# Threshold attention and a feed-forward block on one core: inputs laid out for the matmuls, work moved between engines, batch 0 in half jobs

## The chip, the cores and the metric

The kernel runs on one core of a Trainium2 chip. A core has five engines with a queue of instructions each: TensorE (PE in the profile) multiplies matrices, VectorE (DVE), ScalarE (ACT) and GpSimd (POOL) work elementwise, and SyncE (SP) here issues all the transfers between main memory and the on-chip memory SBUF. Matmul results lie in PSUM, which VectorE and ScalarE can read and GpSimd in this kernel never does. Each engine works off its queue in order. The metric is the device time of one execution in microseconds.

## The reference

Eight batches, eight heads, 576 tokens, 64 values per head. Scores are scaled by 1/8; those more than `tau` = 0.02 under the maximum of their row are dropped before the softmax:

```python
scores = scale * np.matmul(q, k.transpose(0, 1, 3, 2))
thresh = np.max(scores, axis=-1, keepdims=True) - tau
scores = np.where(scores >= thresh, scores, -1000000000.0)
scores = scores - np.max(scores, axis=-1, keepdims=True)
attn = np.exp(scores)
attn = attn / (np.sum(attn, axis=-1, keepdims=True) + 1e-09)
attn_out = np.matmul(attn, v)
```

The heads are put side by side (512 values per token), and a feed-forward block follows, in which each token is mixed with the one before it:

```python
xk = mu_k * x + (1.0 - mu_k) * x_prev
xr = mu_r * x + (1.0 - mu_r) * x_prev
k = np.maximum(xk @ w_k, 0.0)
v = k * k @ w_v
r = 1.0 / (1.0 + np.exp(-(xr @ w_r)))
return r * v
```

`w_k` is 512 x 1024, `w_v` 1024 x 512, `w_r` 512 x 512. The three weights come as 64-bit words of doubles; `mu_r` and `w_r` are about eight times as large as the others, so the gate is sensitive to small errors in attention.

## The kernel before

**Precision by splitting.** TensorE takes one pass over operands of type float32r. To keep near float32 precision an operand x becomes an upper part hi (x rounded to float32r, a ScalarE copy) and a lower part lo = x - hi, and products are summed as hi·hi + hi·lo + lo·hi. Every split costs a copy and a subtraction; where TensorE would be idle, plain float32 matmuls are used instead, which take several passes and need no split (the `whole` job for scores, the `plain` jobs for probabilities by values).

**Jobs and slots.** A job is one batch and two heads; there are 32. It has nine query tiles: four of 128 queries for each head, and one ("T") with the last 64 queries of both heads. Each tile is a slot, so there are 288 slots. A tile runs through a pipeline of five slots:

- `scores` (L308 float32, L326 split): matmuls into the double-buffered PSUM tile `s`, 128 x 576;
- `row_max` (L338, VectorE): the negated maximum of the row; `threshold` (L342, ScalarE): maximum minus tau; `expo` (L346, ScalarE): exponentials into `p`, a tile with three buffers;
- one slot later `mask` (L351, VectorE): p times (s >= threshold), with the sum of the row; `denom` and `inverse` (L355, L358, VectorE): 1e-9 added, reciprocal; `norm` (L361, GpSimd): p times the reciprocal;
- two slots later `turn_p` (L368): five transposes on TensorE into the single PSUM tile `pt`;
- three slots later `p_hi` (L393, or L390 for a plain job; ScalarE) and `p_lo` (L403, VectorE) evacuate `pt` as upper and lower parts into groups of two tiles;
- four slots later `attend` (L439) multiplies a group by the values, or `attend_tile` (L412) one tile of a plain job; `attend_out` (L447, L449, L456) puts the result, transposed, into `xT` or, for the last 64 tokens, `xE`.

**Operands of a job.** While a job runs, the next one's are made: `load` (L158 to L166, eight transfers) and `load_v` (L173, L178, three transfers), transposes of q and k on TensorE (`turn`, L189, nine of them), evacuation with the split (`evac_q`, `evac_k`: ScalarE L206, L209, L219, L222, VectorE L212, L225, GpSimd L210, L223), `stack` (L238 to L241, eight transfers inside SBUF that put upper and lower parts on top of each other), `bd_fill` (L249) and `v_split` (L263, L277, L278). `PREP` tells in which of the nine slots each of these is issued.

**Weights.** Twenty pieces of 128 x 512. `weight_steps` (L128 to L146) turns the words of doubles into float32 with integer operations and splits them, one step a slot and a new piece every second slot from slot 4 on.

**Feed-forward.** Chunks of 256 tokens: two per batch and two for the last 64 tokens of four batches, 18 in all. A chunk has 20 steps on TensorE: eight for `h` (L525, 12 matmuls of 256 columns), four for `z` and eight for `vps` (six of 512 columns each). Ahead of them lie 18 small steps of mixing (`mix`, L485 to L510), in which GpSimd subtracts, adds and splits and ScalarE scales. After each pair of `h` steps `h_out` runs: ReLU (L551, ScalarE), square (L554, VectorE), upper part (L557, ScalarE), lower part (L558, GpSimd).

**The order.** `slot(n)` writes the instructions of one slot in one of two orders (before and from slot `N0` on). ScalarE keeps that written order (`manual_schedule`); the other queues are ordered by the library's scheduler, by its own estimates of durations. How many feed-forward steps go into a slot is a credit: each slot gets `TSLOT` (3.325) minus the estimated TensorE time of its attention work, and each step takes `TSTEP` (1.3) from it; a credit that can't be used is lost. `KEEP` steps stay in hand until the last chunk is ready. A chunk is ready four slots after the last tile of its tokens; the very first chunk then takes eleven slots, one mixing step each, until its steps may begin. What is left after the last slot runs at the end.

## Time and profile before

Three runs: median 1151.09 us, 1151.04 to 1152.42.

| | us | share of the span |
|---|---|---|
| profiled execution, first to last instruction | 1151.2 | |
| median of the runs | 1151.09 | |
| TensorE busy, matmuls (weight loads) | 1104.4 (999.1) | 96% (87%) |
| VectorE busy | 961.3 | 84% |
| ScalarE busy | 846.0 | 73% |
| GpSimd busy | 673.3 | 58% |
| 16 DMA engines, queue 1 | | 38.8% |

The profiled execution is as long as the median run, so durations from it can be put against the median as they are. Busy times overlap and don't add up to the span. Matmuls are pipelined, so the duration in a matmul's row contains time in which the next one already runs. A row of a view by line names the line, the engine, the operation, the tiles (out<-in), the shapes and the count; then the busy time in us and the mean of one in ns; then how long the engine was idle just before these instructions, and what ended that. A row of a timeline starts with its start and length in us.

### The profile page before, as it was taken

The page shows a single profiled execution, that of the slowest core. Times are in us where ns is not written, and L with a number is a line of the kernel's source. Part 1 is how long each engine was busy: PE and PEld are TensorE (multiplying, and loading weights), DVE is VectorE, ACT ScalarE, POOL GpSimd, SP SyncE. Part 2 cuts the span into 40 slices and gives each one's busy share as a digit, 9 for nine tenths or more (in the row PEclk, how much of TensorE's full clock was granted, in tenths as well). Part 3 has the DMA queues.
Part 4 walks back from the last instruction along what each step waited for, and adds up shares of the span by engine and source line. Part 5 has one row for each costly group of instructions (what it writes and reads, how often), then busy time and mean ns, then how long its engine had stood idle before and what let it go on. Part 6 is the DMA issues. An engine that isn't in the chain of part 4 may idle for free.

```text
span 1151.2 us, 22514 instructions
## 1 busy us (share of the span) xinstructions
PE 1104.4 (96%) x7454; PEld 999.1 (87%) x7454; DVE 961.3 (84%) x2399; ACT 846.0 (73%) x1775; POOL 673.3 (58%) x860
## 2 busy tenths in 40 slices
PE   6999989999999999989999999999999999999998
PEld 4887878898989898988989898989898989898997
DVE  3899998888989898988989898989898989895222
ACT  3787877778687878768777878787878787876442
POOL 1465677465656465645747575656565656564672
PEclk9999999999999999999999999999999999999999
DMA  5777334433344344433334444423344444300000
GB/s 131 184 205 204 83 85 93 113 85 74 70 95 105 84 112 95 112 88 71 83 83 104 92 104 104 99 68 87 79 102 94 104 98 99 76 29 13 25 20 18
DMA packets 125027, 105.61 MB, mean 92 GB/s; under 512 B 93681, under 2 KB 101873, under 8 KB 124913
## 3 DMA queue, kind: packets, MB, share of 16 engines
q1 hardware_dynamic: 124912, 104.18, 38.8%
q8 instruction: 60, 0.98, 0.3%
q14 instruction: 55, 0.44, 0.1%
HBM read 39.85 MB, written 9.44 MB: 43 GB/s over the span
## 4 chain that ended last, share of the span: by engine, by line
PE 65%; DVE 18%; ACT 10%; issue 4%; SPq 1%; DMA 1%; POOL 1%; DVEq 0%; ACTq 0%; POOLq 0%
PE h L525 12%; PE vps L525 12%; PE pt L368 10%; PE s L326 9%; PE o L439 9%; PE z L525 8%; DVE p L351 4%; DVE sm L338 3%; DVE plo L403 2%; ACT phi L393 2%; ACT p L346 2%; DVE r L554 2%; PE o L412 1%; DVE phi L403 1%; DVE xT L137 1%
## 5 line engine op out<-in xcount | busy, mean ns | idle before, releaser
L361 POOL TENSOR_SCALAR p<-p,sm 128x576 f32<-128x576 f32 x288 | 222.6, 773 | 255.2 <-DVE sm L358 187.4
L393 ACT ACTIVATE phi<-pt 128x640 fp32r<-128x640 f32 (+1 forms) x270 | 172.4, 649 | 111.3 <-PE pt L368 110.6
L351 DVE SCALAR_TENSOR_TENSOR p<-s,sm,p 128x576 f32<-128x576 f32 x288 | 233.7, 811 | 23.4 <-ACT p L346 19.1
L338 DVE TENSOR_REDUCE sm<-s 128x1 f32<-128x576 f32 x288 | 215.9, 750 | 21.2 <-PE s L308 10.3
L525 PE MATMUL h<-xk,wk 128*128 128x256 f32 x1728 | 231.8, 285 | 1.0 <-ACT r L551 0.3
L525 PE MATMUL vps<-wv,k 128*128 128x512 f32 x864 | 227.2, 399 | 2.0 <-DVE sg L616 1.8
L368 PE MATMUL pt<-ident,p 128*128 128x128 f32 x1440 | 210.4, 276 | 18.6 <-DVE phi L403 8.9
L525 PEld LDWEIGHTS h<-xk,wk 128*128 128x128 f32 x1728 | 216.0, 191 | 4.1 <-ACT r L551 2.1
L346 ACT ACTIVATE p<-s,sm 128x576 f32<-128x576 f32 x288 | 212.6, 738 | 1.4
L368 PEld LDWEIGHTS pt<-ident,p 128*128 128x128 f32 x1440 | 168.2, 142 | 45.9 <-issue 13.5
L403 DVE TENSOR_TENSOR plo<-pt,phi 128x512 fp32r<-128x512 f32 (+1 forms) x270 | 170.5, 632 | 39.6 <-ACT phi L393 33.7
L525 PEld LDWEIGHTS vps<-wv,k 128*128 128x128 f32 x864 | 154.2, 188 | 29.1 <-DVE sg L616 2.9
L439 PE MATMUL o<-phi,vs 128*128 128x256 f32 (+1 forms) x540 | 156.1, 312 | 2.5 <-ACT phi L393 1.6
L439 PE MATMUL o<-plo,vs 128*128 128x256 f32 (+1 forms) x432 | 118.7, 296 | 0.2 <-DVE plo L403 0.2
L326 PE MATMUL s<-st 128*128 128x288 f32 x496 | 112.1, 308 | 5.0 <-DVE p L351 4.2
L558 POOL TENSOR_TENSOR k<-r,k 128x512 fp32r<-128x512 f32 x72 | 93.2, 1295 | 35.6 <-ACT k L557 35.1
L525 PE MATMUL z<-wr,xr 128*128 128x512 f32 x432 | 112.8, 400 | 0.1
L326 PE MATMUL s<-st,st 128*128 128x288 f32 x496 | 107.4, 298 | 0.1
L439 PEld LDWEIGHTS o<-phi,vs 128*128 128x128 f32 x540 | 101.8, 189 | 5.3 <-ACT phi L393 3.3
L342 ACT ACTIVATE sm<-sm,ntau 128x1 f32<-128x1 f32 x288 | 84.5, 293 | 20.8 <-DVE sm L338 19.1
L554 DVE TENSOR_TENSOR r<-r 128x512 f32<-128x512 f32 x72 | 76.8, 1066 | 27.0 <-ACT r L551 26.5
L326 PEld LDWEIGHTS s<-st 128*128 128x128 f32 x496 | 81.8, 191 | 17.4 <-DVE p L351 9.5
(91 smaller groups left out, 1792.5 us busy)
## 6 DMA issues: line engine op xcount, KB each, us to landing
st<-hi SPq DMA_DIRECT2D x62, 288.0 KB, 3.3
st<-lo SPq DMA_DIRECT2D x62, 288.0 KB, 4.1
st<-hi SPq DMA_DIRECT2D x62, 144.0 KB, 3.9
st<-lo SPq DMA_DIRECT2D x62, 144.0 KB, 4.2
raw<-in_q SPq DMA_DIRECT2D x128, 64.0 KB, 2.5
raw<-in_k SPq DMA_DIRECT2D x64, 128.0 KB, 2.9
vraw<-in_v SPq DMA_DIRECT2D x32, 256.0 KB, 2.8
out<-sg SPq DMA_DIRECT2D x32, 256.0 KB, 2.4
```

The costliest lines, as they stand in the source:

```text
L326: PE.matmul(s[:, y, 0:HS], l, r[:, KT + y * HS : KT + (y + 1) * HS], start=(j == 0), stop=(j == n - 1),)
L338: V.tensor_reduce(x["sm"][0], x["s"], axis=AX.XY, op=ALU.max, negate=True)
L346: A.activation(x["p"].rearrange("p (a b) -> p a b", a=2), x["s"], AF.Exp, bias=x["sm"][0])
L351: V.scalar_tensor_tensor(pv, x["s"], thr, pv, op0=ALU.is_ge, op1=ALU.mult, accum_out=sums)
L361: G.tensor_scalar(x["p"], x["p"], x["sm"][3], 0.0, op0=ALU.mult, op1=ALU.add)
L368: PE.transpose(x["pt"][:, c, :], x["p"][:, o : o + P], ident)
L393: A.activation(hi[:, :, off : off + sl.stop - sl.start], x["pt"][:, :, sl], AF.Copy)
L403: V.tensor_tensor(d, x["pt"][0:n, y, sl], hi[0:n, y, cs].bitcast(F32), op=ALU.subtract)
L439: PE.matmul(o[:, 0:n], l, r, start=(j == 0), stop=(j == len(prods) - 1))
L525: PE.matmul(ps, l, r, start=(x == 0), stop=(x == len(prods) - 1))
L554: V.tensor_tensor(r, r, r, op=ALU.mult)
L558: G.tensor_tensor(k2[:, 1, js], r, k2[:, 0, js].bitcast(F32), op=ALU.subtract)
```

## The change

**Layout.** The arrays are rearranged before the launch. `qk` holds for each batch and pair of heads a 128 x 1152 tile: the two heads' values on the rows, and on the columns the 576 queries, the last 64 keys and the first 512 keys, already transposed. `load` is one transfer, and the nine transposes of q and k with their evacuation are gone. In their place `scale` (ScalarE, in place over the 576 query columns), `upper` (ScalarE, 1152 columns) and two `lower` (GpSimd, 576 columns each) work on SBUF. The tokens of a tile now lie in order, so the outputs into `xT` are contiguous. `v` is one transfer into a buffer of its own tag, `mu` is one small transfer at the start, and each piece of the weights is contiguous.

**Moves between engines.** `threshold` goes from ScalarE to GpSimd; the square in `h_out` from VectorE to ScalarE (`Square`); the clamp of the weights (s2) and the lower parts of q and k from VectorE to GpSimd.

**Sums inverted in pairs.** Two tiles share a tile of statistics. `inverse` handles both sums at once, after the mask of the odd one, and then both `norm` follow. The even tile's normalization thereby comes one slot later than before, in the slot at whose end `turn_p` transposes it.

**Half jobs.** Batch 0's four jobs become eight: first four with the four tiles of the first 256 queries of both heads, then four with the other five tiles. Each half job loads and stacks q, k and v in full. The first chunk is ready at slot 19 instead of 34, `N0` is 20 instead of 36, the weights start every 1.5 slots from slot 2, the plain jobs are four half jobs instead of five whole ones, and `TSLOT` is 3.15.

```diff
-    TSLOT, TSTEP, KEEP, N0 = 3.325, 1.3, 10, 36
-    PLAIN, WHOLE = 5, 1
+    TSLOT, TSTEP, KEEP, N0 = 3.15, 1.3, 10, 20
+    PLAIN, WHOLE, HALF = 4, 1, 1
...
         def s2():
             t = box["t"]
-            V.tensor_scalar(t, t, W_MIN, W_MAX, op0=ALU.max, op1=ALU.min)
+            G.tensor_scalar(t, t, W_MIN, W_MAX, op0=ALU.max, op1=ALU.min)
...
     def load(job):
+        raw = p1.tile([P, W], F32, tag="raw", name="raw")
+        SY.dma_start(raw, qk[job["b"], job["hp"]])
         job["raw"] = raw
...
     def load_v(job):
+        vraw = p1.tile([P, 2, 5, D], F32, tag="vraw", name="vraw")
+        SY.dma_start(vraw, v[job["b"], job["hp"]].rearrange("p (h c d) -> p h c d", h=2, c=5))
+        job["vraw"] = vraw
...
+        def scale():
             if job["whole"]:
                 job["qk"] = p3.tile([P, W], F32, tag="st1", name="qk")
+                A.activation(job["qk"][:, 0:S], raw[:, 0:S], AF.Copy, scale=qscale)
+                V.tensor_copy(job["qk"][:, S:W], raw[:, S:W])
+                return
+            A.activation(raw[:, 0:S], raw[:, 0:S], AF.Copy, scale=qscale)
+
+        def upper():
+            if job["whole"]:
                 return
             box["hi"] = p1.tile([P, W], FR, tag="hi", name="hi")
+            A.activation(box["hi"], raw, AF.Copy)
+
+        def lower(y):
             if job["whole"]:
                 return
+            if y == 0:
+                box["lo"] = p1.tile([P, W], FR, tag="lo", name="lo")
+            cs = slice(y * S, (y + 1) * S)
+            G.tensor_tensor(box["lo"][:, cs], raw[:, cs], box["hi"][:, cs].bitcast(F32), op=ALU.subtract)
...
     def row_max(x):
-        sm = p3.tile([P, 4], F32, tag="sm", name="sm", bufs=8)
-        x["sm"] = [sm[:, j : j + 1] for j in range(4)]
+        n = x["n"]
+        if n % 2 == 0 or n == 0:
+            x["sm2"] = p3.tile([P, 4, 2], F32, tag="sm", name="sm", bufs=5)
+        else:
+            x["sm2"] = slots[n - 1]["sm2"]
+        x["sm"] = [x["sm2"][:, j, n % 2 : n % 2 + 1] for j in range(4)]
         V.tensor_reduce(x["sm"][0], x["s"], axis=AX.XY, op=ALU.max, negate=True)
 
     def threshold(x):
         nmx, thr, _, _ = x["sm"]
-        A.activation(thr, nmx, AF.Identity, bias=ntau, scale=-1.0)
+        G.tensor_scalar(thr, nmx, -1.0, ntau, op0=ALU.mult, op1=ALU.add)
...
     def inverse(x):
-        V.reciprocal(x["sm"][3], x["sm"][2])
+        sm = x["sm2"]
+        V.tensor_scalar(sm[:, 2], sm[:, 2], 1e-9, None, op0=ALU.add)
+        V.reciprocal(sm[:, 3], sm[:, 2])
...
                 r = p2.tile([P, 2, CH], F32, tag="r_sb", name="r")
-                A.activation(r, st[("h", j)], AF.Relu)
-                def rest():
-                    V.tensor_tensor(r, r, r, op=ALU.mult)
-                    def split():
+                A.activation(r, h, AF.Relu)
+                def split():
+                    A.activation(r, r, AF.Square)
                     A.activation(k2[:, 0, js], r, AF.Copy)
                     G.tensor_tensor(k2[:, 1, js], r, k2[:, 0, js].bitcast(F32), op=ALU.subtract)
...
-        for hp in range(NPAIR):
+        for part in range(2) if b < HALF else (None,):
+            for hp in range(NPAIR):
+                ji = len(jobs)
+                tiles = full if part is None else full[5 * part - part : 4 + 5 * part]
...
     PREP = {
-        0: (["q_turn", "q_evac"], []),
-        2: (["k_turn", "k_evac"], []),
-        4: (["t_turn", "t_evac"], ["stack0"]),
-        5: (["load"], ["stack1", "v0"]),
+        0: (["scale", "upper"], []),
+        1: (["lower0"], []),
+        2: (["lower1", "stack0"], []),
+        4: (["v0", "stack1"], ["load"]),
         8: ([], ["bd"]),
     }
+    PREP_HALF = {
+        0: (["scale", "upper"], ["lower0"]),
+        1: (["lower1", "stack0"], ["stack1", "load"]),
+        2: (["v0"], []),
+        3: ([], ["bd"]),
     }
...
+    wstart = [2 + 3 * j // 2 for j in range(len(wjobs))]
...
+        def pair_norm():
+            if x1 is not None and x1["n"] % 2 == 1:
+                inverse(x1)
+                norm(x2)
+                norm(x1)
...
         if n < N0:
             on(x, row_max)
             on(x1, mask)
             flush_a()
-            on(x1, denom)
-            on(x1, inverse)
+            pair_norm()
             on(x3, p_hi)
-            on(x1, norm)
             on(x, threshold)
             on(x, expo)
```

`stack(y)` now handles the upper parts of both heads (y = 0) or the lower parts (y = 1), four transfers each.

More of the change, by code (lines that the diff above doesn't have):

```diff
@@ L244, in bd_fill @@
         def bd_fill():
-            if job["whole"]:
+            if job["whole"] or not job["tail"]:
                 return
@@ L258, in v_split @@
         def v_split(h):
+            vraw = job["vraw"]
             if job["plain"]:
@@ L282, in prep_steps @@
         return dict(
[L283 to L288 removed]
+            scale=scale,
+            upper=upper,
+            lower0=lambda: lower(0),
+            lower1=lambda: lower(1),
             stack0=lambda: stack(0),
@@ L431, in attend @@
     def attend(job, h, g):
-        n = 2 * P + (ST if job["tg"] == g else 0)
+        n = 2 * P + (ST if job["tail"] and job["tg"] == g else 0)
         hi, lo = job["groups"][(h, g)]
@@ L635, in tile_threshold_attention_then_rwkv_ffn @@
     for b in range(B):
-        for hp in range(NPAIR):
-            ji = len(jobs)
-            jobs.append(
-                dict(b=b, hp=hp, tiles=full, tg=1, groups={}, plain=ji < PLAIN, whole=ji < WHOLE)
-            )
+        for part in range(2) if b < HALF else (None,):
+            for hp in range(NPAIR):
+                ji = len(jobs)
+                tiles = full if part is None else full[5 * part - part : 4 + 5 * part]
+                jobs.append(
+                    dict(
+                        b=b,
+                        hp=hp,
+                        tiles=tiles,
+                        tg=0 if part == 0 else 1,
+                        tail=part != 0,
+                        groups={},
+                        plain=ji < PLAIN,
+                        whole=ji < WHOLE,
+                    )
+                )
     slots = []
@@ L756, in tile_threshold_attention_then_rwkv_ffn @@
     for ji, job in enumerate(jobs[:-1]):
-        for off, plan in (PREP0 if ji == 0 else PREP).items():
+        half = len(job["tiles"]) < 9
+        for off, plan in (PREP_HALF if half else PREP).items():
+            off = len(job["tiles"]) - 1 if "bd" in plan[1] else off
             prep_at.setdefault(starts[ji] + off, []).append((ji + 1, plan))
@@ L795, in tensor_time @@
             for ji, h, g in groups:
-                pe += 9 * (2 * P + (ST if jobs[ji]["tg"] == g else 0)) * 0.425e-3
-            for _, plan in steps:
-                pe += 0.435 * sum(nm.endswith("turn") for nm in plan[0])
+                pe += 9 * (2 * P + (ST if jobs[ji]["tail"] and jobs[ji]["tg"] == g else 0)) * 0.425e-3
             if n + 1 < NS:
```

219 lines of the change are left out of this document (70 added, 149 removed).

## The prediction

> **What bounds the kernel now.** I read the page first, then the busy time by stage, then the rows of single engines.
>
> ```profile
> span 1151.2 us, 22514 instructions
> PE 1104.4 (96%) x7454; PEld 999.1 (87%) x7454; DVE 961.3 (84%) x2399; ACT 846.0 (73%) x1775; POOL 673.3 (58%) x860
> PE 65%; DVE 18%; ACT 10%; issue 4%; SPq 1%; DMA 1%; POOL 1%; DVEq 0%; ACTq 0%; POOLq 0%
> ```
>
> A busy share of 96% on TensorE isn't yet a limit, because matmuls overlap and the ends are modelled. Its real price is the distance between starts. The timeline of the tail, where TensorE runs alone, gives it:
>
> ```profile
> 1079.89 11.04 PE L525 MATMUL vps<-wv,k 128*128 128x512 f32 x48
> 1090.77 11.68 PE L525 MATMUL h<-xk,wk 128*128 128x256 f32 x96
> 1102.28 5.63 PE L525 MATMUL z<-wr,xr 128*128 128x512 f32 x24
> 1107.75 11.04 PE L525 MATMUL vps<-wv,k 128*128 128x512 f32 x48
> 606.11 0.71 PE L368 MATMUL pt<-ident,p 128*128 128x128 f32 x5
> 607.73 0.43 PE L326 MATMUL s<-st 128*128 128x288 f32 x2
> ```
>
> From the first start to the last, 27.86 us pass for a chunk's 20 steps: 1.393 us a step. The 96 matmuls of 256 columns take 0.120 each. Five transposes in 0.71, the last alone 0.27, are 0.11 each; two score matmuls in 0.43, one 0.30, are 0.13. A job of nine slots has 40 score matmuls (5.3 us), 45 transposes (4.9), 36 value matmuls of 256 or 320 columns (4.8, at 0.120 and 0.147 by width) and nine transposes of q and k (1.0): 1.77 us a slot. The credit rule adds 11 feed-forward steps to nine slots (1.70), so TensorE needs 3.47.
>
> The stages (engine busy time by window; the cuts are the 36th and 45th exponential, the last exponential, the end):
>
> ```profile
> core 0: us, PE busy (x) PEld busy (x) DVE busy (x) ACT busy (x) POOL busy (x), PEclk, DMA share, GB/s
> 0.00:132.00 132.00, 116.42 (x732) 96.52 (x732) 106.08 (x257) 88.73 (x200) 62.16 (x91) 0.99 0.67 176
> 132.00:161.60 29.60, 24.39 (x165) 21.53 (x165) 27.50 (x60) 26.48 (x62) 21.11 (x25) 0.94 0.37 81
> 161.60:1048.00 886.40, 864.95 (x5976) 793.33 (x5977) 804.18 (x2052) 688.69 (x1441) 535.54 (x687) 1.00 0.39 88
> 1048.00:1151.20 103.20, 98.65 (x583) 87.70 (x581) 23.58 (x32) 42.06 (x75) 54.45 (x60) 1.00 0.07 21
> ```
>
> The long stage holds 243 slots: 3.64 us each. VectorE is busy 3.31 of them (91%), ScalarE 2.83, GpSimd 2.20. So two engines stand almost equally close to the slot: TensorE needs 3.47, VectorE 3.31, and their hand-overs cost the rest. In the first stage no feed-forward step runs, and VectorE's own work sets the pace. In the tail, 59 steps by the credit rule, 59 x 1.393 = 82 us, TensorE alone counts.
>
> **VectorE after the change.** These are its groups, kept apart by shape:
>
> ```profile
> L351 DVE SCALAR_TENSOR_TENSOR p<-s,sm,p 128x576 f32<-128x576 f32 x288 | 233.7, 811 | 23.4 <-ACT p L346 19.1
> L338 DVE TENSOR_REDUCE sm<-s 128x1 f32<-128x576 f32 x288 | 215.9, 750 | 21.2 <-PE s L308 10.3 <-PE s L326 8.9
> L403 DVE TENSOR_TENSOR plo<-pt,phi 128x512 fp32r<-128x512 f32 x216 | 147.7, 684 | 35.3 <-ACT phi L393 32.8
> L403 DVE TENSOR_TENSOR phi<-pt,phi 64x128 fp32r<-64x128 f32 x216 | 61.3, 284 | 4.7
> L554 DVE TENSOR_TENSOR r<-r 128x512 f32<-128x512 f32 x72 | 76.8, 1066 | 27.0 <-ACT r L551 26.5
> L358 DVE RECIPROCAL sm<-sm 128x1 f32<-128x1 f32 x288 | 45.6, 158 | 5.1
> L355 DVE TENSOR_SCALAR sm<-sm 128x1 f32<-128x1 f32 x288 | 41.8, 145 | 2.0
> L212 DVE SCALAR_TENSOR_TENSOR lo<-pq,qscale,hi 128x512 fp32r<-128x512 f32 x31 | 23.2, 748 | 0.9 <-ACT hi L206 0.2
> L225 DVE TENSOR_TENSOR lo<-pk,hi 128x512 fp32r<-128x512 f32 x31 | 21.3, 688 | 1.2 <-ACT hi L219 0.5
> ```
>
> Out go the squares (76.8 us), the lower parts of q and k (44.5) and half of the additions and reciprocals (43.7): 165 us. Per slot of the long stage that is 11/9 x 8/20 x 1.066 / 2 = 0.26 for squares (one per two h steps), 0.16 and 0.15, together 0.57, of which some 0.09 was overlap. VectorE's need falls from 3.31 to 2.83; at the 91% that it reached, a slot could be 3.1.
>
> **TensorE after.** The transposes of q and k go: 3.47 - 0.11 = 3.36, say 3.37 with the credit rule's rounding, still 11 steps per nine slots (3.15 instead of 3.325 of credit, with 0.145 less charged). So now TensorE paces by itself, 0.27 above VectorE. Before, its loss was 0.17 a slot beside a VectorE only 0.16 lower. Nothing shows what is left; it lies between 0 and the old 0.17, unless a new wait comes. I take 0.07, nearer to the low end because the second engine moves away. A paced slot: 3.44.
>
> **GpSimd and ScalarE take the work.**
>
> ```profile
> L342 ACT ACTIVATE sm<-sm,ntau 128x1 f32<-128x1 f32 x288 | 84.5, 293 | 20.8 <-DVE sm L338 19.1
> L551 ACT ACTIVATE r<-h 128x512 f32<-128x512 f32 x72 | 42.8, 594 | 34.7 <-PE h L525 34.4 <-POOL vs L278 0.3
> L361 POOL TENSOR_SCALAR p<-p,sm 128x576 f32<-128x576 f32 x288 | 222.6, 773 | 255.2 <-DVE sm L358 187.4 <-PE s L326 39.3 <-PE o L439 16.6
> L558 POOL TENSOR_TENSOR k<-r,k 128x512 fp32r<-128x512 f32 x72 | 93.2, 1295 | 35.6 <-ACT k L557 35.1
> L858 POOL TENSOR_SCALAR xE<-xT 128x4 f32<-128x4 f32 x8 | 1.6, 204 | 4.7 <-DVE xT L449 2.5 <-ACT xT L429 2.2
> ```
>
> GpSimd gets the threshold (0.2 a slot by the 128x4 row) and two subtractions of 128x576 a job (1295 x 576/512 = 1.46 each, 0.32 a slot), less the two 64-column ones (0.07): 2.20 + 0.45 = 2.65 of 3.44, 77%. The two normalizations, now back to back every second slot, add none. ScalarE loses the threshold (0.29) and seven copies per job out of PSUM; it gains per job one scale and one upper part of 1152 columns, and the squares (0.59 by the Relu row, 72 of them, 0.17 a slot): 2.83 or a little less, 80%. Both are covered while they stay under 3.44. What stands behind a late threshold is the mask on VectorE, and behind that the next scores, which need the mask's PSUM buffer.
>
> Against this move speaks the Trainium skill, "Perfetto Trace Analysis", Optimizing Scalar/DVE Operations: GpSimd and VectorE share a read port, so offloading between them may not help. The trace agrees for the square, the merge of the weights' words and others with two SBUF inputs, and does not for the mask, which has one (duration ns, min/median/max):
>
> ```profile
> L554 DVE TENSOR_TENSOR r<-r x72: 672/1074/1714, 170.7 to 1131.0; 128x512 f32<-128x512 f32 x72
> L137 DVE SCALAR_TENSOR_TENSOR xT<-wv_words,xT x8: 693/917/1760, 117.5 to 163.9; 128x512 uint32<-128x512 uint32 x8
> L351 DVE SCALAR_TENSOR_TENSOR p<-s,sm,p x288: 791/812/821, 15.2 to 1047.2; 128x576 f32<-128x576 f32 x144
> ```
>
> By that rule the moved work would come back as stalls on VectorE, and the sum would be that of the second rival.
>
> **The start.** Batch 0 runs as eight half jobs, so its first chunk is ready after slot 19 instead of 34; eleven slots of mixing follow, and the steps begin in slot 31 instead of 46. But the next chunks come at 39 and 70, as before. By the credit rule slots 54 to 71 hold four steps, and seven each fall into 99 to 107 and 135 to 143: in 36 slots TensorE waits for chunks and VectorE's 3.1 counts.
>
> In slots 0 to 35 VectorE pays for the rest (its groups in that window, by shape):
>
> ```profile
> L136 DVE TENSOR_SCALAR xT<-xT 128x512 uint32<-128x512 uint32 x15 | 10.0, 670 | 0.0
> L132 DVE TENSOR_SCALAR xT<-xT 128x512 f32<-128x512 f32 x15 | 6.6, 437 | 0.0
> L137 DVE SCALAR_TENSOR_TENSOR xT<-wk_words,xT 128x512 uint32<-128x512 uint32 x8 | 7.4, 928 | 0.0
> L138 DVE SCALAR_TENSOR_TENSOR xT<-wk_words,xT 128x512 uint32<-128x512 uint32 x8 | 6.3, 786 | 0.0
> ```
>
> A piece costs 0.67 + 0.93 + 0.79 = 2.4 us, and the clamp (0.44) goes to GpSimd. All 20 pieces fall into these slots, not 15: +12. Only 16 slots are plain, not 45, so 18 tiles need the split of the probabilities (0.68 + 0.28): +17, and eight merges as long as the split's smaller part or twice that +4. Out: the clamps 6.6, half the additions and reciprocals 5, four jobs' lower parts of q and k 5.7. Net +16. The first scores start after three landings and nine transposes:
>
> ```profile
> 5.77 1.21 PE L189 MATMUL pq<-ident,raw 128*128 128x128 f32 x4 [5.77 <-DMA raw<-in_q]
> 10.29 2.29 PE L308 MATMUL s<-qk 64*128 64x288 f32 x4 [0.66 <-DVE qk L216]
> ```
>
> One load and one pass of ScalarE beside one of VectorE take their place. The gain lies between 0 (a load nine times as large lands later) and 4.5 (no time after the landing); I take 1. Stage end: 132 + 16 - 1 = 147. The DMAs nearly double per slot here, since a half job loads and stacks as much as a whole one: five jobs' operands become nine, 0.9 MB of loads and 1.8 MB of stacked halves each, and four more pieces of 0.5 MB. That makes 23 MB some 35. At 176 GB/s for a share of 0.67 the engines' limit is 263 GB/s, so 35 MB take 133 of the 147 us: hidden, with little to spare. Were the cover gone, a half job of four slots would wait for its stacked halves; the upper end of the range holds that. SP issues ten transfers per job instead of nineteen.
>
> **The sum**, against the span of 1151.2 (the median is 1151.09): 147 + 216 x 3.44 (743) + 36 x 3.1 (112) + five slots that drain (16) + 64 steps left over by the credit rule (89) + 4 for the last gate and store = **1111 us**, 3.5% less.
>
> **The rivals.**
> *TensorE without losses* (17%): 3.37 a slot and a first stage hidden as before (132): 1081. For it: VectorE has 0.3 spare. Against: ScalarE, too, stands between TensorE's steps, and waits for its transposes:
>
> ```profile
> ACT phi L393 <- PE pt L368: 110.6, 129, 3.3
> ```
>
> *VectorE stalled by GpSimd's reads* (13%): 40 weight merges at 1.4 instead of 0.9 in the first stage: 1131. For: the row that reached 1760 ns. Against: after these slots no frequent instruction of VectorE has two SBUF inputs.
> *The order loses as before* (12%): 0.17 to 0.20 a slot: 1132 to 1139.
> *The threshold on GpSimd paces* (12%): it queues behind subtractions of 1.3 to 1.46; at 77% busy, with half an instruction to wait, 0.45 + 0.2 join VectorE's loop, and the pair of normalizations delays the transposes: 3.1 + 0.65 = 3.75 in all 252 slots: 147 + 945 + 109 = 1201, slower. It decides from a mean slot of 3.55 on, (1151 - 147 - 109)/252; with 3.6 it is 1163. For: GpSimd's queue is in order, and the threshold had ScalarE's place just ahead of the exponential. Against: VectorE can mask late by the 0.3 that it gained.
> *Square reloads ScalarE's table* (3%), as Sigmoid does:
>
> ```profile
> L590 ACT ACT_TABLE_LOAD x15 | 19.2, 1283 | 0.3
> L346 ACT ACT_TABLE_LOAD x14 | 18.0, 1283 | 0.1
> ```
>
> Two loads around each of 72 squares are 185 us, 0.7 a slot, which brings ScalarE to 3.4 and the slot, with the old 0.17, to 3.6: 1163. Against: Relu and Copy, its neighbours, load none.
>
> *No visible difference* (3%): gains and the longer start cancel.
>
> **Chances.** The forecast itself 40%, its own range 1090 to 1128. About 0.2% is what a measurement of this kernel can tell from nothing. Faster 0.82, same 0.03, slower 0.15. The range reaches down to the loss-free case with some of VectorE's bounds (1075) and up to the old losses with a stalled first stage (1152).
>
> **What would show it.** Right: the exponentials 243 slots long stand 3.4 apart, VectorE's busy share there falls to about 83%, GpSimd's rises to 77%, the first feed-forward matmul lies near 130 us, the first stage ends near 147, and the last exponential comes near 1000. Wrong: long waits of the mask for the threshold, table loads beyond 30, slots of 3.6, or a stretch near slots 54 to 71 as slow as its neighbours.

## The result, and the profile after

The changed kernel takes **1291.01 us** (median of four runs, 1288.82 to 1291.98) against 1151.07 before (1148.3 to 1152.42): 1.122 times as long, 95% interval 1.1195 to 1.124. The forecast was 1111.

The top of the page of the changed kernel: span, busy time of the engines, and in 40 slices of 32 us the busy tenths of TensorE and GpSimd, the clock granted to TensorE, and the transfers:

```profile
span 1289.8 us, 21010 instructions
PE 1115.0 (86%) x6984; PEld 988.4 (77%) x6984; DVE 890.4 (69%) x2046; ACT 854.1 (66%) x1435; POOL 855.9 (66%) x1188
PE   5575456888798998899999999999998989899998
POOL 3676789666467675767566767786767676656662
PEclk9766577999799999999999989999999999999999
DMA  7665533323333333233333334333333323310000
```

TensorE falls from 96% busy to 86%, and VectorE, which was to be relieved, has 71 us less to do and idles through them. In slices 2 to 7 something shows that the kernel before hardly had: the granted clock is down to 0.5 to 0.7.

Busy time by stage, with the cuts at the start of the 37th, the 73rd and the last exponential; first the kernel after, then the one before with its own cuts:

```profile
core 0: us, PE busy (x) PEld busy (x) DVE busy (x) ACT busy (x) POOL busy (x), PEclk, DMA share, GB/s
0.00:236.00 236.00, 145.17 (x665) 123.62 (x666) 132.06 (x268) 109.25 (x189) 167.72 (x187) 0.72 0.50 143
236.00:369.00 133.00, 110.63 (x678) 96.07 (x677) 104.36 (x250) 85.53 (x143) 76.60 (x122) 0.92 0.35 86
369.00:1177.40 808.40, 751.80 (x5013) 673.14 (x5012) 641.49 (x1504) 603.11 (x1009) 553.82 (x816) 0.99 0.35 85
1177.40:1289.80 112.40, 107.40 (x635) 95.55 (x634) 12.53 (x26) 56.25 (x98) 57.80 (x65) 0.99 0.06 20
```

```profile
0.00:132.20 132.20, 116.42 (x732) 96.52 (x732) 106.27 (x257) 88.93 (x200) 62.36 (x91) 0.99 0.67 176
264.50:1045.60 781.10, 763.52 (x5271) 700.70 (x5270) 711.57 (x1821) 609.84 (x1272) 469.29 (x605) 1.00 0.39 88
```

The first 36 slots take 236 us instead of 132, and that is three quarters of the loss. The 215 slots from the 73rd exponential to the last take 808.4 instead of 781.1 (3.76 us each instead of 3.63), and the tail 112 instead of 106.

Five rows of the changed kernel's waits (engine and line, what it waited for, total us, times, longest), then two of the kernel before:

```profile
ACT phi L351 <- PE pt L326: 200.4, 153, 4.3
DVE plo L361 <- ACT phi L351: 115.6, 128, 3.5
PEld pt L326 <- POOL p L319: 106.7, 92, 5.4
PE pt L326 <- POOL p L319: 71.7, 59, 5.2
DVE xT L136 <- POOL xT L132: 42.7, 16, 7.0
```

```profile
PEld pt L368 <- POOL p L361: 8.6, 14, 1.5
PE pt L368 <- POOL p L361: 4.5, 6, 1.4
```

In the third and fourth rows TensorE waits for the normalization on GpSimd ahead of its transposes, 106.7 and 71.7 us where the kernel before waited 8.6 and 4.5. The last row, VectorE waiting for the clamp of a weight piece on GpSimd, is new. The first two rows (110.6 and 33.7 us before) are what the late transposes pass on.

**The clamp.** All instructions of L132, after and before (count, then duration min/median/max in ns):

```profile
L132 POOL TENSOR_SCALAR xT<-xT x20: 1913/1915/2397, 35.9 to 218.0; 128x512 f32<-128x512 f32 x20
```

```profile
L132 DVE TENSOR_SCALAR xT<-xT x20: 407/419/1164, 38.8 to 161.7; 128x512 f32<-128x512 f32 x20
```

The same max and min over 128x512 floats take 1.9 us on GpSimd, 4.6 times VectorE's 0.42. The timeline of the changed kernel shows who stands behind them (start, duration, idle time before and its releaser in brackets):

```profile
33.01 2.77 POOL L185 TENSOR_TENSOR lo<-raw,hi 128x576 fp32r<-128x576 f32 x2
...
35.87 3.79 POOL L132 TENSOR_SCALAR xT<-xT 128x512 f32<-128x512 f32 x2
...
37.82 0.82 DVE L136 TENSOR_SCALAR xT<-xT 128x512 uint32<-128x512 uint32 x1 [5.98 <-POOL xT L132]
...
38.56 0.81 DVE L311 SCALAR_TENSOR_TENSOR p<-s,sm,p 128x576 f32<-128x576 f32 x1
...
39.52 0.82 PE L280 MATMUL s<-st 128*128 128x288 f32 x2 [3.53 <-DVE p L311]
```

GpSimd works through two lower parts and then two clamps. VectorE's next instruction, L136, needs the clamped piece and blocks its queue for 5.98 us; the mask behind it comes late, and TensorE waits 3.53 us for the mask, which holds the scores' PSUM buffer.

**The pair.** A stretch of the long stage in the same view:

```profile
715.02 0.80 DVE L311 SCALAR_TENSOR_TENSOR p<-s,sm,p 128x576 f32<-128x576 f32 x1
...
716.42 0.58 DVE L315 TENSOR_SCALAR sm<-sm 128x2 f32<-128x2 f32 x1
...
717.52 0.15 DVE L316 RECIPROCAL sm<-sm 128x2 f32<-128x2 f32 x1
...
718.44 1.49 POOL L319 TENSOR_SCALAR p<-p,sm 128x576 f32<-128x576 f32 x2
...
719.26 0.77 PE L326 MATMUL pt<-ident,p 128*128 128x128 f32 x5 [0.75 <-POOL p L319]
...
720.06 0.70 ACT L351 ACTIVATE phi<-pt 128x640 fp32r<-128x640 f32 x1 [2.65 <-PE pt L326]
```

The mask at 715.02 is that of the odd tile. Only behind it do the shared addition and reciprocal run, then the even tile's normalization, and the even tile's transposes follow the moment it ends, late. From the trace, over slots 72 to 287: an even tile's normalization starts 5.65 us after its own mask has ended, its transposes 0.39 us after the normalization, and TensorE idles 0.38 us just before them (41 us in all). An odd tile's starts after 2.69 us, with 3.11 to spare. In the kernel before both kinds start after 1.6 us and have 3.9 to spare.

### The profile page after: what moved, and what is told of

The parts are those of the page before. It is cut to its first block, busy times and chain, and to the rows that moved or that the text cites. A ratio compares the mean times of both kernels' runs of the same rounds, so it can differ in the third digit from the quotient of the medians.

```text
span 1289.8 us, 21010 instructions
## 1 busy us (share of the span) xinstructions
PE 1115.0 (86%) x6984; PEld 988.4 (77%) x6984; DVE 890.4 (69%) x2046; ACT 854.1 (66%) x1435; POOL 855.9 (66%) x1188
## 5 line engine op out<-in xcount | busy, mean ns | idle before, releaser
L351 ACT ACTIVATE phi<-pt 128x640 fp32r<-128x640 f32 (+1 forms) x304 | 193.0, 646 | 202.0 <-PE pt L326 200.4
L326 PE MATMUL pt<-ident,p 128*128 128x128 f32 x1440 | 230.5, 294 | 100.4 <-POOL p L319 71.7
L326 PEld LDWEIGHTS pt<-ident,p 128*128 128x128 f32 x1440 | 175.3, 150 | 148.4 <-POOL p L319 106.7
L361 DVE TENSOR_TENSOR plo<-pt,phi 128x512 fp32r<-128x512 f32 (+1 forms) x304 | 192.0, 632 | 118.8 <-ACT phi L351 115.6
L481 PE MATMUL h<-xk,wk 128*128 128x256 f32 x1728 | 240.9, 289 | 4.1 <-ACT xk L463 2.5
L481 PEld LDWEIGHTS h<-xk,wk 128*128 128x128 f32 x1728 | 223.4, 195 | 5.6 <-ACT xk L463 2.7
L302 POOL TENSOR_SCALAR sm<-sm,ntau 128x1 f32<-128x1 f32 x288 | 80.8, 281 | 156.5 <-DVE sm L298 86.0
L395 PE MATMUL o<-phi,vs 128*128 128x320 f32 (+1 forms) x600 | 179.1, 318 | 3.4 <-ACT phi L351 3.2
L395 PE MATMUL o<-plo,vs 128*128 128x320 f32 (+1 forms) x480 | 142.7, 316 | 3.6 <-DVE plo L361 3.0
L395 PEld LDWEIGHTS o<-phi,vs 128*128 128x128 f32 x600 | 117.4, 196 | 7.0 <-ACT phi L351 5.8
L185 POOL TENSOR_TENSOR lo<-raw,hi 128x576 fp32r<-128x576 f32 x70 | 99.7, 1433 | 11.2 <-ACT hi L177 11.0
```

The source lines that it names most:

```text
L185: G.tensor_tensor(box["lo"][:, cs], raw[:, cs], box["hi"][:, cs].bitcast(F32), op=ALU.subtract)
L326: PE.transpose(x["pt"][:, c, :], x["p"][:, o : o + P], ident)
L351: A.activation(hi[:, :, off : off + sl.stop - sl.start], x["pt"][:, :, sl], AF.Copy)
L361: V.tensor_tensor(d, x["pt"][0:n, y, sl], hi[0:n, y, cs].bitcast(F32), op=ALU.subtract)
L395: PE.matmul(o[:, 0:n], l, r, start=(j == 0), stop=(j == len(prods) - 1))
L481: PE.matmul(ps, l, r, start=(x == 0), stop=(x == len(prods) - 1))
```

## The experiments

Each run is the changed kernel with edits. The table shows the end of the first 36 slots, the mean slot from there to the 72nd and on to the last exponential, and the part of the first 36 slots at half TensorE clock, all from the traces. Of the experiments only e9, e14 and e16 were executed more than once (four, four and five times); the other times are of one execution each, while those of the kernel before lay between 1148.3 and 1154.3 us over all its executions. So a difference of a few us between two such runs is not shown.

| run | what differs from the changed kernel | us | first 36 end | slots 36-71 | slots 72-287 | half clock |
|---|---|---|---|---|---|---|
| before | | 1151 | 132 | 3.68 | 3.63 | 3 |
| changed | | 1291 | 236 | 3.71 | 3.76 | 133 |
| e1 | clamp on VectorE | 1258.4 | 205 | 3.69 | 3.75 | 92 |
| e2 | whole jobs | 1226.7 | 159 | 4.09 | 3.75 | 38 |
| e3 | whole jobs, clamp on VectorE | 1204.8 | 140 | 3.91 | 3.77 | 10 |
| e4 | sums tile by tile | 1227.2 | 230 | 3.27 | 3.56 | 130 |
| e5 | addition in two instructions | 1290.2 | 237 | 3.68 | 3.75 | 147 |
| e9 | e3 and sums tile by tile | 1135.3 | 128 | 3.53 | 3.57 | 0 |
| e10 | half jobs, clamp on VectorE, sums tile by tile | 1197.7 | 200 | 3.31 | 3.55 | 92 |
| e11 | e9, threshold on ScalarE | 1131.3 | 127 | 3.58 | 3.54 | 0 |
| e12 | e10, scores in float32 | 1180.8 | 183 | 3.30 | 3.56 | 68 |
| e13 | e4, normalizations issued in pairs | 1227.1 | 228 | 3.31 | 3.56 | 116 |
| e14 | layout alone | 1144.8 | 125 | 3.67 | 3.60 | 0 |
| e15 | e9, weights every 1.5 slots | 1141.0 | 144 | 3.33 | 3.55 | 17 |
| e16 | e11, scores of batch 0 in float32 | 1128.3 | 125 | 3.56 | 3.54 | 0 |
| e17 | e10, filler on TensorE | 1211.8 | 211 | 3.37 | 3.56 | 38 |
| e18 | e10, probabilities of batch 0 in float32 | 1173.7 | 173 | 3.40 | 3.55 | 38 |
| e19 | e18 and e12 | 1153.8 | 151 | 3.43 | 3.56 | 10 |

**e1, the clamp back on VectorE**

```diff
-            G.tensor_scalar(t, t, W_MIN, W_MAX, op0=ALU.max, op1=ALU.min)
+            V.tensor_scalar(t, t, W_MIN, W_MAX, op0=ALU.max, op1=ALU.min)
```

> The changed kernel with one line back: the clamp of the weights on VectorE. Theory C (the clamp, 1.9 us on GpSimd against 0.42 on VectorE, stands in GpSimd's queue ahead of thresholds and normalizations, and VectorE's queue waits 42.7 us for it ahead of masks): the first 36 slots fall from 236 to 165-190 us, the total to 1220-1245. Theory H (half jobs: operands of a job of four slots come too late, whoever clamps): the first 36 slots stay above 215, the total above 1270. The slots from 36 on stay at 3.73 us by both.

1258.4: 33 us come back, 31 of them in the first 36 slots. That stage still takes 205, which lies between the ranges of the two theories: the clamp is a part of the loss and not its main part.

**e2 and e3, batch 0 in whole jobs**, without and with that clamp:

```diff
-    TSLOT, TSTEP, KEEP, N0 = 3.15, 1.3, 10, 20
-    PLAIN, WHOLE, HALF = 4, 1, 1
+    TSLOT, TSTEP, KEEP, N0 = 3.15, 1.3, 10, 36
+    PLAIN, WHOLE, HALF = 5, 1, 0
...
-    wstart = [2 + 3 * j // 2 for j in range(len(wjobs))]
+    wstart = [4 + 2 * j for j in range(len(wjobs))]
```

> The changed kernel with batch 0 in whole jobs, and with N0 = 36, five plain jobs and a piece of the weights every second slot as in the kernel before; the moves between engines, the layout and the pairs stay, the clamp on GpSimd too. Theory H: the first 36 slots fall to 130-150 us and the total to 1185-1205. Theory C: clamps every second slot still block, the first 45 slots take 190 us or more, total 1215-1250.

> The run before it (whole jobs in batch 0) with the clamp on VectorE as well. Both theories: the first 36 slots near 125-135 us. What is left against the kernel before is then the slots behind them: at the changed kernel's 3.73 us a slot the total is 1165-1185; had half jobs or clamps also slowed the later slots, 1120-1145.

1226.7 and 1204.8. The half jobs, with the order that belongs to them, cost most of the first stage (236 to 159), and the clamp another 19 there. By the bounds set e2 fits theory C: its first 45 slots take 203 us, where they take 178 in e3, so with whole jobs, too, the clamp on GpSimd blocks. But it is worth 22 us there and the half jobs 64. e3 misses its expectation: 140 and 1204.8 us are above all the ranges given, since its later slots are no shorter than the changed kernel's. The slots from the 72nd on stay at 3.75 to 3.77: their loss has another cause.

**e4, sums inverted and normalized tile by tile**

```diff
-            if x1 is not None and x1["n"] % 2 == 1:
+            if x1 is not None:
                 inverse(x1)
-                norm(x2)
                 norm(x1)
...
-        V.tensor_scalar(sm[:, 2], sm[:, 2], 1e-9, None, op0=ALU.add)
-        V.reciprocal(sm[:, 3], sm[:, 2])
+        sums = x["sm"][2]
+        V.tensor_scalar(sums, sums, 1e-9, None, op0=ALU.add)
+        V.reciprocal(x["sm"][3], sums)
...
```

Each tile also has its own tile of statistics again.

> The changed kernel with the sums inverted tile by tile again, each tile normalized in the slot after its own, all else as changed. Theory P (the even tile's normalization, a slot later and two in a row, makes TensorE wait for p: 178 us of its idle time is put down to the normalization): the slots from 36 on fall from 3.73 to 3.45-3.6, total 1240-1265, and TensorE's wait for the normalization falls below 60 us. Rival (the wait is GpSimd's load, not the pairing): 3.7 stays, total 1280-1300.

1227.2: 64 us back, and here the late slots do fall, from 3.76 to 3.56, those from 36 to 71 from 3.71 to 3.27. An even tile's normalization now starts 1.94 us after its mask, and TensorE's wait for it shrinks from 106.7 us (weight loads) and 71.7 (matmuls) to 13.5 for the matmuls and, for the weight loads, to this row of the waits of e4:

```profile
PEld pt L322 <- POOL p L315: 29.8, 27, 6.0
```

So the pairing is the cause of the slower long stage. The place of the loss is in the traces too: the 41 us that TensorE idles directly ahead of the even tiles' transposes from slot 72 on are 5 in e4, and these 36 us are most of the 43 by which that stage is longer (0.2 us in 216 slots).

**e5, why the pairing loses: the addition in two instructions**

```diff
-        V.tensor_scalar(sm[:, 2], sm[:, 2], 1e-9, None, op0=ALU.add)
+        for y in range(2):
+            V.tensor_scalar(sm[:, 2, y : y + 1], sm[:, 2, y : y + 1], 1e-9, None, op0=ALU.add)
```

> The changed kernel with one edit: the addition of 1e-9 to the two columns of sums is made in two one-column instructions instead of one; the reciprocal and the two normalizations stay paired. Theory P1 (the pairing loses because the two-column addition on VectorE stretches beside GpSimd's work: mean 396 ns where one column took 145): the additions come back to about 145 ns each, VectorE's busy time falls by some 16 us, and the slots from the 72nd on fall from 3.76 to about 3.60 us; some 1250 us in all. Theory P2 (it loses because the first tile of each pair gets its normalization a slot later, so that its transposes and the plan behind them wait on GpSimd): the additions get shorter but those slots stay at 3.72 to 3.78 us, and the time at 1280 to 1292.

The additions in the changed kernel, with their reciprocals, and in e5 (groups of VectorE by shape):

```profile
L315 DVE TENSOR_SCALAR sm<-sm 128x2 f32<-128x2 f32 x144 | 57.0, 396 | 1.5
L316 DVE RECIPROCAL sm<-sm 128x2 f32<-128x2 f32 x144 | 23.0, 160 | 2.6
```

```profile
L316 DVE TENSOR_SCALAR sm<-sm 128x1 f32<-128x1 f32 x288 | 42.2, 147 | 3.3
```

The two-column addition is odd by itself: median 169 ns, mean 396, longest 1357, where one column never takes more than 157. The trace shows what stretches it: 54 of the 144 take over 250 ns, each of them starts while an instruction of GpSimd runs, and 53 end 15 to 40 ns after an instruction of GpSimd has ended. In e5, 179 of the 288 one-column additions start beside a running instruction of GpSimd too, and none is stretched. But e5's edit makes the addition short again, and the time doesn't move (1290.2, slots of 3.75). So the stretched addition isn't what costs the time. What remains of the pair in e5 is the reciprocal that needs both masks, and with it the late start of the even tile's normalization.

**e13, is it the order on GpSimd alone?** Sums are inverted one by one, but both normalizations are written behind the odd tile's inversion.

```diff
             if x1 is not None:
                 inverse(x1)
-                norm(x1)
+                if x1["n"] % 2 == 1:
+                    norm(x2)
+                    norm(x1)
```

> The changed kernel with each sum inverted by itself as soon as its mask is done, but the two normalizations on GpSimd still issued together after the odd tile's inversion. So the paired instructions on VectorE are gone and only the lateness and the bunching on GpSimd are left. Theory L (the lateness of the even tile's normalization, just ahead of its transposes, is the whole loss of the pairing): the slots from the 72nd on stay at 3.70 to 3.78 us and the time at 1275 to 1295. Theory V (it is the paired instructions on VectorE, which wait for two masks): these slots fall to 3.60 or less, the time to 1225 to 1245.

1227.1, as e4. By the numbers that is theory V, but the trace takes the test away: the library's scheduler orders GpSimd's queue by its own estimates, and the normalizations stand where they stand in e4, one by one, 1.95 us after their masks. The run repeats e4. What it does show is that the written place of a normalization doesn't matter here, and the data that it needs do.

**e9 and e10, the three causes apart.** e9 is e3 with e4's edit, e10 is e1 with e4's edit.

> The changed kernel with three edits together: batch 0 in whole jobs (order and spacing of the weight jobs as before the change), the clamp back on VectorE, sums inverted and normalized tile by tile. What is left of the change: the new layout of q, k, v, the threshold and the lower split on GpSimd, the Square on ScalarE. Theory A (the three causes are separate and add up: 64 us from the half jobs, about 19 to 33 from the clamp, 64 from the pairing): the first 36 slots end near 138 us, later slots take 3.5 to 3.56, and the time is 1120 to 1145, under the kernel before. Theory B (the work moved to GpSimd loses by itself, and the three only add to it): later slots stay over 3.65 and the time is above 1155.

> The changed kernel with the clamp on VectorE and sums inverted tile by tile, batch 0 still in half jobs with weights every one and a half slots. Theory H (the half jobs by themselves starve the first 36 slots): these end at 190 to 205 us as with the clamp alone, later slots take 3.5 to 3.56, the time is 1185 to 1200. Theory C (the half jobs lose only together with the clamp and the pairing): the first 36 slots end under 160 us and the time is under 1160.

e9 takes 1135.25 us (1134.28 to 1135.81), 0.985 of the kernel before (interval 0.9832 to 0.9874): what is left of the change is a gain. e10 takes 1197.7. From 1291 the steps are 64 for the pair (e4), 30 for the clamp (e10) and 62 for the half jobs with their order (e9). The first stage and the long stage of e9, then the first of e10:

```profile
0.00:128.00 128.00, 106.87 (x683) 88.19 (x683) 101.32 (x247) 84.62 (x148) 87.75 (x129) 1.00 0.61 181
...
255.00:1021.40 766.40, 742.58 (x5020) 669.56 (x5019) 634.87 (x1716) 603.00 (x1009) 554.05 (x815) 1.00 0.37 90
```

```profile
0.00:200.40 200.40, 133.02 (x664) 114.76 (x665) 152.16 (x324) 109.34 (x189) 131.95 (x167) 0.77 0.58 168
```

VectorE has 152 us of work in e10's first 36 slots and 101 in e9's, GpSimd 132 and 88. A small part of that is the clamp again: it is no longer short on VectorE either (a mean of 0.86 us in e10, 0.47 in the kernel before). By the trace 13 of e10's 20 clamps take over 0.5 us, and each of these started while an instruction of GpSimd ran and ended 0.28 to 0.29 us after it:

```profile
L132 DVE TENSOR_SCALAR xT<-xT 128x512 f32<-128x512 f32 x20 | 17.2, 858 | 1.3 <-ACT xT L128 1.2
```

**e15, e12, e18, e19: what in the half jobs.** e15 is e9 with the changed kernel's weight pace; e12 is e10 with the scores of all eight half jobs in float32, so that nothing of their operands is split or stacked; e18 is e10 with the probabilities of all eight half jobs in float32, and with them the values, which then aren't split either; e19 is both.

```diff
-    wstart = [4 + 2 * j for j in range(len(wjobs))]
+    wstart = [2 + 3 * j // 2 for j in range(len(wjobs))]
```

```diff
-    PLAIN, WHOLE, HALF = 4, 1, 1
+    PLAIN, WHOLE, HALF = 4, 8, 1
```

```diff
-    PLAIN, WHOLE, HALF = 4, 1, 1
+    PLAIN, WHOLE, HALF = 8, 1, 1
```

```diff
-    PLAIN, WHOLE, HALF = 4, 1, 1
+    PLAIN, WHOLE, HALF = 8, 8, 1
```

> As the run with whole jobs, clamp on VectorE and tile by tile sums (1135 us, first 36 slots 128 us), but the weight pieces come every one and a half slots, as in the changed kernel, instead of every second. If the pieces' pace is part of what starved the half jobs' slots, the first 36 slots now end above 145 us; if the half jobs' own operands are the cause, they end at 128 to 138 us and the time is 1135 to 1145.

> As the run with half jobs, clamp on VectorE and tile by tile sums (1197.7 us, first 36 slots 200 us), but all eight half jobs multiply their scores in plain float32, as the first does: their operands are scaled and no more, with no upper and lower parts, no halves stacked by transfers. Theory S (what starves the half jobs is the chain from the landed operands over ScalarE, GpSimd and the stacking transfers to the scores, too long for four slots): the first 36 slots end at 125 to 145 us, the time is 1120 to 1145. Theory W (what starves them is the transfers' volume with weight pieces every one and a half slots, and the copies of v that wait for them): the first 36 slots still take over 165 us, the time is above 1165.

> As the run with half jobs, clamp on VectorE and tile by tile sums, but the probabilities of all eight half jobs are multiplied by the values in plain float32, not only of four: the 18 tiles after the 16th (the 20th slot on) need no upper and lower part on ScalarE and VectorE. If the split of the probabilities starves the stage, the first 36 slots end at 150 to 180 us instead of 200 and the time falls by 20 us or more; if it doesn't, 195 us or more and a time within 8 us of 1197.7.

> As the run before in this list, and the scores of all eight half jobs in plain float32 too, so that neither operands nor probabilities are split in batch 0. If half jobs as such (twice the loads of k, twice the copies of v, for the same tiles) are the cause, the first 36 slots still take 165 us or more. If the splits are, they end at 125 to 155 us and the time is 1125 to 1155.

The first 36 slots end at 144 (e15), 183 (e12), 173 (e18) and 151 (e19). The faster weights cost this stage 16 us, of which 7 come back in the next 36 slots. Net of TensorE's longer float32 matmuls, splitting and stacking the operands every four slots costs this stage 18 us with the probabilities split (e10 to e12) and 22 without (e18 to e19); splitting the probabilities of the last four half jobs costs it 28 (e10 to e18) or 32 (e12 to e19).

The ends of the stage aren't quite like for like. By the traces ten feed-forward steps run in the first 36 slots of e10 and e12, six in those of e18 and e19, and none with whole jobs; at the prediction's 1.39 us a step, ten are an estimated 14 us of work that is only brought forward. In the whole time the operands cost 17 and 20 us, the probabilities 24 and 27. With neither split, e19 is 7 us behind e15 at the end of the stage and 13 in the whole time, and e15 still splits the operands of three whole jobs there, which e16 below prices at 2. So neither theory of e12 was enough by itself: of the 62 us of the half jobs, the larger part is the two splits that fall into the first 36 slots, and a smaller part is the halving as such with the faster weights.

**e17, is the halved clock the carrier?** In the runs above, the longer the first stage, by and large, the longer its time at half clock. Of the 174 stretches at half clock in all the traces, 168 follow 3.4 us in which TensorE was busy for 0.6 or less, and the other six follow 0.61 to 0.73. The reverse doesn't hold: after 80 windows under 0.6 the clock stayed full. e17 is e10 with throw-away work:

```diff
         x["pt"] = ps_t.tile([P, 5, P], F32, tag="pt", name="pt")
+        for c in range(15 if x["n"] < 36 else 0):
+            PE.transpose(x["pt"][:, c % 5, :], ident, ident)
```

> As the run with half jobs, clamp on VectorE and tile by tile sums (1197.7 us; first 36 slots 200 us, 92 of them at half TensorE clock), and TensorE makes 15 throw-away transposes of the identity matrix ahead of the transposes of each of the first 36 tiles, into the same PSUM tile, which the real ones then overwrite: some 1.65 us more work a slot at full clock, 59 us in all, which can run while TensorE waits for the normalized tile. Theory K (the halved clock carries the loss: an idle TensorE is clocked down, works at half speed and delays the others, so that it idles again): the time at half clock falls under 30 us and the first 36 slots end at 150 to 180 us, though TensorE does more. Theory M (the halved clock only marks the waiting, and the chain of operands sets the time): the half clock may go, but the first 36 slots still end at 195 us or later.

The time at half clock in the first 36 slots falls from 92 to 38 us, and they still end at 211 instead of 200. By the bounds set, the half clock marks the waiting more than it carries it. This isn't clean: up to the 21st tile e17 is ahead (98 against 104 us, with an estimated 30 us of extra work), after it behind, and the filler can itself stand in front of the transposes. How many of the 72 us between e9 and e10 the halved clock adds stays open.

**e11 and e14, what the moved work is worth.** e11 is e9 with the threshold back on ScalarE; e14 also has the square and the lower parts back on VectorE, so that of the change the layout alone is left.

```diff
-        G.tensor_scalar(thr, nmx, -1.0, ntau, op0=ALU.mult, op1=ALU.add)
+        A.activation(thr, nmx, AF.Identity, bias=ntau, scale=-1.0)
```

```diff
-            G.tensor_tensor(box["lo"][:, cs], raw[:, cs], box["hi"][:, cs].bitcast(F32), op=ALU.subtract)
+            V.tensor_tensor(box["lo"][:, cs], raw[:, cs], box["hi"][:, cs].bitcast(F32), op=ALU.subtract)
...
-                    A.activation(r, r, AF.Square)
+                    V.tensor_tensor(r, r, r, op=ALU.mult)
```

> As the run with whole jobs, clamp on VectorE and tile by tile sums, and the threshold back on ScalarE. Theory T (288 thresholds of 0.28 us on GpSimd delay the long mask and the normalizations behind it): the slots from the 72nd on are 0.05 to 0.12 us shorter than in that run, 10 to 25 us in all. Theory N (the threshold on GpSimd is covered, since the long mask waits for it only 6.7 us in all in the changed kernel; ScalarE's share would grow by some 0.2 us a slot instead): within 5 us of that run, or longer.

> Only the new layout of q, k, v is left of the change: whole jobs, tile by tile sums, clamp, square and the lower parts of q and k on VectorE, the threshold on ScalarE. Theory M (the moved work frees VectorE and thereby shortens the slots): the slots from the 72nd on take 3.62 or more, and the time is 1145 to 1160, 10 us or more above the run with whole jobs, clamp on VectorE and tile by tile sums (1135). Theory Z (TensorE's own work with its hand-overs sets the slot, so that only the transposes that the layout removes count, and the moves are worth nothing): slots of 3.53 to 3.58, the time within 8 us of 1135.

e11: 1131.3 in one execution, 4 us under e9, so no gain from the threshold on GpSimd is shown. e14: 1144.82 (1143.12 to 1146.23), 0.994 of the kernel before (0.9917 to 0.9961). The layout is worth some 7 us, and square and lower parts another 13 (e14 to e11): slots of 3.60 against 3.54. Both theories of e14 were half right: the moves count, but bring only an eighth of the 99 us that they take off VectorE (960.1 to 861.5).

**e16, the version that this points to**: e11 with the scores of all four jobs of batch 0 in float32.

```diff
-    PLAIN, WHOLE, HALF = 5, 1, 0
+    PLAIN, WHOLE, HALF = 5, 4, 0
```

> As the run with whole jobs, clamp on VectorE, tile by tile sums and the threshold on ScalarE (1131.3 us), and all four jobs of batch 0 multiply their scores in plain float32, which leaves their upper and lower parts and stacking transfers out of the first 36 slots. If that chain still costs there, the first 36 slots end at 115 to 124 us instead of 127 and the time is 1118 to 1129; if TensorE's longer float32 matmuls cost as much, 127 us or more and 1130 to 1138. Either way it is under both kernels.

1128.32 us (1127.9 to 1129.3), 0.979 of the kernel before (0.9776 to 0.9803): the fastest of all. The first 36 slots end at 125, 2 us before e11's and just outside the range set for a gain, while the time lies inside it. TensorE's matmuls are busy for 113.5 us of them where e11's are for 108.5, so the longer float32 matmuls may have paid back the rest; no run separates that.

## Why the prediction was wrong

Of the 179 us between the forecast and the profiled execution, 89 lie in the first 36 slots (236 for 147), 87 in the slots from there to the last exponential (941.5 for 743 + 112), 3 in the tail. Of the 87 some 30 are the pace that TensorE keeps without the pairing (3.58 for 3.44 in 216 slots), the other 57 nearly all the pairing.

- **"The two normalizations, now back to back every second slot, add none."** This step failed. It counted GpSimd's time and not whom they release, so the delay was put at nothing: the even tile's inversion waits for the odd tile's mask, which moves its normalization 3.7 us later (5.65 against 1.94 in e4) and uses up the slack ahead of its transposes. The pairing costs 64 us.
- **"Half of the additions and reciprocals (43.7)"** was mis-sized. L315 and L316 take 57.0 + 23.0 = 80.0 us where one by one they took 87.4, a saving of 7. The two-column addition waits for GpSimd, as e5's section shows. That fits the Trainium skill, "VectorE: DVE Perf Modes", Mode 2×_2P: an instruction with a single source, in SBUF like its output, reads its tensor in two halves through both read ports where its outermost dimension longer than one is even (or odd and equal in source and output), and by the same page, section "Two Vector instructions with no wait between them", what is read through the second port is read through an interface shared with GpSimd. A single column has no such dimension. The durations agree for the addition (longest 1357 ns against 157); the reciprocal of two columns stays at a mean of 160. And e5 shows that the stretching cost no time.
- **"The clamp (0.44) goes to GpSimd"** had a price for what VectorE loses and none for what GpSimd gains. It measures 1.98 us a piece, 39.5 us in all, on the path through L136, the mask and the scores: 30 to 33 us with half jobs. The forecast had no max or min of GpSimd among its rows and took no bound for it.
- **"Stage end: 147 ... hidden, with little to spare"** failed most. The transfers were counted well (33.65 MB in the first 236 us for "some 35"), and their volume wasn't the limit: the DMA engines were busy for half of these 236 us. The price that was missed was the chain of a half job: scale, upper and lower parts, stacking, every four slots instead of nine, which was taken as covered and costs the stage 18 to 22. The split of the probabilities, put at 21 with its merges, costs it 28 to 32; the weights' pace, put at 12, costs 16. VectorE's own work in the stage, put at 16 more than before, came to 26 more (132 for 106). The stage also had the clock at half for 133 us, which the forecast had no term for; the kernel before gave it little sign of that (0.99 in its first stage, 0.94 in its second). How much the clock itself cost stays open (e17). "The upper end of the range holds that" was wrong by far.
- **"A paced slot: 3.44."** With pairing off the slots outside the starved stretches take 3.58 (e4). The loss beside TensorE's own need, "between 0 and the old 0.17", came out a little above that, at 0.21, although VectorE has 0.6 us a slot to spare (634.87 us busy of 766.40 in 215 slots of e9). So the rival "the order loses as before", with its 0.17 to 0.20, was nearly right in this term. What the 0.2 consists of isn't shown.
- **"36 chunk-starved slots x 3.1"** was right in mechanism and size: in e4 slots 54 to 71, 99 to 107 and 135 to 143 take 3.07, 3.23 and 3.23, with 5, 8 and 8 feed-forward steps by the trace (forecast: 4, 7 and 7). In the changed kernel the pair hides most of it (3.61, 3.40, 3.55).
- **The rival of 1201 us** gave 3.75 a slot, and the slots from the 72nd on take 3.76, but that match is luck, for its main mechanism isn't there. The mask waits for the threshold 6.7 us in all, and moving the threshold back (e11) yields 4 us, little more than executions differ. Its side remark, that the pair of normalizations delays the transposes, was the cause, and it should have been a rival of its own.
- **The rival of stalled merges** (1131 us) didn't come: the 40 merges of the weights take a mean of 0.89 us where the kernel before had 0.99, and not 1.4.
- **Right as they stood:** the square on ScalarE (0.63 us for 0.59) with no further table loads (30 before and after), the lower parts (1.43 for 1.46), the layout's 0.11 a slot off TensorE, the first feed-forward step about where it was put (slot 28 for 31, though at 179 us for 130), the tail (112 for 109). VectorE did get free time, and little behind it needed it: 13 us (e14 to e11).

The waits of the mask for the threshold, which the prediction named as its first sign of failure:

```profile
L311 DVE SCALAR_TENSOR_TENSOR p<-s,sm,p 128x576 f32<-128x576 f32 x288 | 234.4, 814 | 72.2 <-ACT p L306 57.7 <-POOL sm L302 6.7 <-issue 1.6
```

## What to carry to other kernels

An instruction that serves two items starts when the later one is ready: before pairing, look up how much slack the earlier item has at its consumer, not how much the pairing saves. When work moves to another engine, price it there from a row of the same operation on that engine, and if there is none, measure it by itself before it is put in front of a queue that others wait for. When a stage is cut finer to start something earlier, count each fixed step of a piece once per piece, since a step hidden under nine slots isn't hidden under four.

## What the runs showed of the hardware

- A max and min over 128x512 floats takes 1.91 to 2.40 us on GpSimd (changed kernel) and at its shortest 0.41 on VectorE (kernel before), while a multiply and add over 128x576 takes a mean of 0.76 on GpSimd. The Trainium skill, "GPSIMD Engine Reference", Engine selection, puts instructions of GpSimd with one input at roughly the line rate; for this operation these runs disagree.
- A two-column addition on VectorE took up to 1357 ns in the changed kernel, the long ones ending with an instruction of GpSimd (53 of 54), and a one-column one at most 157 in e5. The clamp on VectorE took 0.40 to 1.60 us in e10, the long ones again ending shortly after an instruction of GpSimd.
- TensorE's clock was granted at half in stretches of 3.4 us and their multiples: 133 us of the changed kernel's first 236, 0 of e9's first 128. The changed kernel's 20 stretches each follow 3.4 us with TensorE 0.05 to 0.61 busy; the most in any trace was 0.73 (e19). The Trainium skill, "TensorE: Matmul & The Clock Gate", What's actually happening, describes such a window of about 3.4 us; the lengths here agree. Its account asks for an idle window, and here windows that were half busy were often enough.
